# Splitting the first MLP chunk's operands during attention, and weaving the last mixing by a list

## The chip, the cores and the metric

The kernel runs on one core of a Trainium2 chip. The metric is the device time of one execution in microseconds. The engines are named as in the profile: PE (TensorE, matrix products) with PEld (its weight loads), DVE (VectorE), ACT (ScalarE), POOL (GpSimd) and SP (SyncE, which here only issues DMAs).

## The reference

Random-feature attention, then a token-mixing and channel MLP block, all in float32 (the MLP's weights arrive as float64).

```python
def phi(x):                       # x = q or k, scaled by D ** -0.25
    h = einsum('bhsd,md->bhsm', x, omega) - sum(x * x) / 2
    return exp(h - max(h)) / sqrt(m)
kv = einsum('bhsm,bhsd->bhmd', phi(k), v);  z = sum(phi(k), axis=2)
attn = einsum('bhsm,bhmd->bhsd', phi(q), kv) / (phi(q) . z + 1e-6)

x = attn as (8, 576, 512)
u = x + ((x.transpose(0, 2, 1) @ U) @ V).transpose(0, 2, 1)     # "mixing": U (576, 32), V (32, 576)
out = u + relu(u @ w_ch1) @ w_ch2                                # w_ch1 (512, 2048), w_ch2 (2048, 512)
```

Batch 8, 8 heads, 576 tokens, head width 64, 128 features.

## The kernel before, in words

Products of the MLP and of the feature projection are made from two-part operands: a high half (a copy to the type fp32r, on ACT) and a low half (the rest, a subtraction on DVE or POOL). Three products replace one: high x high, high x low, low x high. "Splitting" a tile means making these two halves; the function `split` (L735 to L738) does it in the MLP.

**Attention** (L638 to L720) is one software pipeline of 16 rounds of 9 steps, plus 7 steps to drain it; `s` is the step. A step handles one tile of 128 rows for two parts, a key unit and a query unit: project (PE, L528 to L530), row maximum `nm` (DVE, L536), exponentials `e` (ACT, L543), then kv products for keys (L440), or transposes (L466), a copy `eT` (L471) and the products with kv (L479, L486) for queries; `finish` divides and writes the result into the tile `x` (L496 to L511). The loads of a round are issued one round earlier by SP: `kt` and `qt`, 8 DMAs each (L381), and the values (L423, L427).

Four pairs of batches are formed. When a pair's x is complete, a generator `mixing` (L279) is put in a queue and advanced twice per step. It makes `py` (5 tiles, twice; PE L327) from the halves `mh` (ACT, L290) and `ml` (POOL, L291), copies it as `y` (ACT L330, DVE L332), then per tile a second product `ph` (`spread`, PE L302, L299), adds x (`add`, DVE L306, into one of two tiles `ut`) and stores the row tile u to device memory (SP, L312). The last pair's generator is not finished when attention ends.

A second generator, `decoding` (L106), turns the float64 words of U, V and the MLP's weights into float32 during attention: a load (three ahead), one or two ACT operations, five DVE operations (L142 to L150) and one on POOL (L167) per job. It is advanced in two steps of three until ten jobs are through (`left`). The rest of it is advanced in the first MLP chunk.

The **MLP** runs over chunks of token tiles: chunk 0 has six (768 tokens), the next ones four. Chunk 0 is computed plainly: for each of 16 slices f of the hidden width, `whole1` (L863) makes the first layer (12 products 512 wide and 12 products 256 wide, L876), `relu` the two halves of the activation (L885, L886), and `second` (L935) the second layer (L951). Chunks 1 and up use seven products per block pair in place of eight (`products`, L925).

In between stands the turn that the change touches. During attention the first six row tiles of u are loaded back transposed in blocks (`ahead`, L617; DMA L353) into four tiles and turned on DVE (`turn_ahead`, L627) into `uT` and three-buffered `us`. After attention (L987 to L999):

```python
weave()
ws[0] = Halves(0, nc.vector)      # split the first weights: ACT and DVE
one.whole(0)                      # split u, part 0: ACT and DVE
while not hold[0]:                # advance the last mixing to its 8th py tile
    weave()
for i in range(1, NC):
    one.whole(i)                  # split u, parts 1 to 3
for x in first_left:
    one.short(x)                  # split the 256 further tokens: ACT and POOL
```

and then the first pass, with one step of the mixing after each group of three products, the second with two (`twice`), and `settle` (L1006), which ends the mixing and frees its memory. Instructions wrapped in `tc.keep_in_program_order` (short: `keep`, `order`) are issued in the written order on their engine; others may be reordered by the scheduler, which orders by its own model of times when the program is built. Each engine works its list in order.

Of the kernel before, what the change touches and what calls it, by code (L numbers as in the profile page):

```python
# [9 lines left out]
F32 = mybir.dt.float32  # L10
F32R = mybir.dt.float32r
# [3 lines left out]
ALU = mybir.AluOpType  # L15
# [14 lines left out]
def performer_mlp_kernel(ctx: ExitStack, tc, q, k, v, omega, U, V, w1, w2, out):  # L30
# [27 lines left out]
    def f32(ap):  # L58
        return ap.bitcast(F32)
# [28 lines left out]
    tp = ctx.enter_context(tc.tile_pool(name="tp", bufs=1))  # L88
# [177 lines left out]
    left = [6 + 5 * EARLY]  # L266
# [10 lines left out]
    hold = [False]  # L277

    def mixing(pair, x, last):  # L279


        xs, ys, sums, stores = {}, [], {}, []
        rest = nc.gpsimd
        order = tc.keep_in_program_order if last else lambda step: step

        def prep(t):
            if t < NT:
                xh = mp.tile([P, DM], F32R, name="mh", bufs=2)
                xl = mp.tile([P, DM], F32R, name="ml", bufs=2)
                order(nc.scalar.copy(out=xh, in_=x[:, t, :]))  # L290
                order(rest.tensor_tensor(out=xl, in0=x[:, t, :], in1=f32(xh), op=ALU.subtract))  # L291
                xs[t] = (xh, xl)

        def spread(t):
            bank = "p_kv" if last and t % 2 else "p_m"
            sums[t] = ps.tile([P, DM], F32, name="ph", tag=bank)
            if t == 4:
                for b in range(2):
                    nc.tensor.matmul(sums[t], svm[:, b, :], ys[b], start=(b == 0), stop=(b == 1))  # L299
            else:  # L300
                b, r = divmod(t * P, S)
                nc.tensor.matmul(sums[t], sv[:, r : r + P], ys[b], start=True, stop=True)  # L302

        def add(t):
            ut = mp.tile([P, DM], F32, name="ut", tag="ut", bufs=2)
            order(nc.vector.tensor_tensor(out=ut, in0=sums.pop(t), in1=x[:, t, :], op=ALU.add))  # L306
            stores.append((u_rows(pair * NT + t), ut))

        def store():
            if stores:  # L310
                o, i = stores.pop()
                order(nc.sync.dma_start(out=o, in_=i))  # L312

        prep(0)
        yield
        yield
        for b in range(2):
            py = ps.tile([P, DM], F32, name="py", tag="p_m")
            for t in range(4 * b, 4 * b + 5):
                store()  # L320
                if (b, t) != (0, 4):
                    prep(t + 1)
                hold[0] = last and b == 1 and t > 6
                yield
                w = su[:, t + b, :, :].rearrange("p a r -> p (a r)")
                for i in range(2):
                    nc.tensor.matmul(py, w, xs[t][i], start=(t == 4 * b and i == 0), stop=(t == 4 * b + 4 and i == 1))  # L327
                yield
            y = mp.tile([P, DM], F32R, name="y", tag="y", bufs=2)
            order(nc.scalar.copy(out=y, in_=py))  # L330
# [12 lines left out]
        yield  # L343
        yield
        store()
# [268 lines left out]
    AFTER = 88  # L614
    first_uT, first_left, first_raw = [], [], {}

    def ahead(i):  # L617

        i //= 4
        if i == 0:  # L620
            first_uT.append(tp.tile([P, NC, TOK], F32, name="uT"))
        if i % 2 == 0:
            first_left.append(tp.tile([P, 2, TOK // 2], F32, name="us", bufs=3))
        first_raw[i] = rawp.tile([P, ends[0] * P], F32, name=f"raw{i}")
        fetch(0, {i: first_raw[i]})

    def turn_ahead(i):  # L627
        i, over = divmod(i, 2)
        o, x = first_uT[0][:, i, :], first_raw[i][:, :TOK]
        if over:  # L630
            o, x = first_left[i // 2][:, i % 2], first_raw[i][:, TOK:]
        tc.keep_in_program_order(nc.vector.transpose(o, x))

    steps = {}
    decoder = decoding([u_job(), *v_jobs(), *weight_jobs()], 6, EARLY)
    mixers = []
    x = None
    for s in range(NR * NT + 7):  # L638
# [17 lines left out]
        if AFTER <= s < AFTER + 4 * NC and (s - AFTER) % 4 == 0:  # L656
            ahead(s - AFTER)
# [60 lines left out]
        if mixers:  # L718
            next(mixers[0], 0)
        steps.pop(s - max(DELAY.values()), None)  # L720
# [6 lines left out]
    rows_out = out.rearrange("b s c -> (b s) c")  # L727
    up = ctx.enter_context(tc.tile_pool(name="up", reuse_waits="tile", bufs=2))
# [66 lines left out]
    class Halves:  # L795


        def __init__(self, f, rest=nc.gpsimd):
            self.ops = []
            for d in range(2):  # L800
                self.ops.append(weight_tile())
                split(self.ops[-1], w1f[:, 2 * d : 2 * d + 2, f * P : (f + 1) * P], rest)

    class Chunk:
        def __init__(self, c, raws=None):
            self.c, self.raws, self.turned, self.ops, self.s = c, raws or {}, 0, [], {}
            self.n = ends[c] - first[c]
            self.u, self.po = {}, None
            self.uT = tp.tile([P, NC, TOK], F32, name="uT") if c else first_uT[0]
            self.half = []  # L810

# [14 lines left out]
        def slot(self):  # L826
            self.ops.append(up.tile([P, 2, 2, HT], F32R, name="ux", bufs=8))
            return self.ops[-1]

        def whole(self, i):  # L830

            split(self.slot(), self.uT[:, i, :].rearrange("p (k t) -> p k t", k=2), nc.vector)

        def short(self, x, rest=nc.gpsimd):

            self.half.append(up.tile([P, 2, 2, HT], F32R, name="ux", bufs=8))
            split(self.half[-1], x, rest)
# [15 lines left out]
        def add(self):  # L853
# [5 lines left out]
            split(self.slot(), x, nc.gpsimd if self.c == 1 and i in (3, 5) else nc.vector)  # L859
# [127 lines left out]
    weave = lambda: next(mixers[0], None)  # L987
    while left[0] > 0:
        advance(decoder)
    weave()  # L990
    ws[0] = Halves(0, nc.vector)
    one.whole(0)
    while not hold[0]:
        weave()
    for i in range(1, NC):
        one.whole(i)
    for x in first_left:
        one.short(x)
    g = one.whole1(ws.pop(0), lambda: 1 in ws or ws.update({1: Halves(1)}), weave)  # L999
    late = {}  # L1000

    def twice():
        weave()
        weave()
# [11 lines left out]
    def whole_pass(chunk, g, each):  # L1016


        for f in range(NF):
# [3 lines left out]
            if f + 1 < NF:  # L1023
                places = iter(range(4))
                opening = chunk is one and f == 0
                g = chunk.whole1(ws.pop(f + 1), lambda: each(f, next(places)), twice if opening else lambda: None)
# [126 lines left out]
```

## Time and profile before

| | us |
|---|---|
| median of 3 runs | 1107.28 (1104.17 to 1108.17) |
| the profiled execution | 1106.08 |
| its span on the core | 1104.3 |
| mean granted PE clock | 0.992 |
| attention, first projection to last product | about 9 to 316 |
| the turn | about 316 to 341 |
| chunk 0, f = 2 and on | 344 to 461 |
| the other chunks | 461 to the end |

Rows of the profile are read thus: start, duration, engine, line, operation, output<-inputs, tile size and, in brackets, the idle time of that engine just before it with what ended it. "SPq" is SP's DMA issue. The windows give, for a stretch, its length, the busy time of each engine with the number of instructions, the granted PE clock (1.00 is full), the DMA engines' busy share and GB/s. PE's products overlap, so the distance between two starts, not the duration, is what a product costs.

### The profile page before, as it was taken

How to read it: one execution, taken by the hardware profiler on the slowest of the kernel's cores; microseconds unless marked ns; L12 is line 12 of the kernel's file. 1: busy time of each engine (PE TensorE's matmuls, PEld its weight loads, DVE VectorE, ACT ScalarE, POOL GpSimd, SP SyncE). 2: the span in 40 equal slices, each digit the busy share in tenths (PEclk: the TensorE clock that was granted, in tenths of full speed). 3: DMA queues.
4: the chain of work that ended last, by engine and by line, in shares of the span. 5: the costliest groups of instructions: out<-in, count | busy, mean ns of one | idle time of the engine just before them, and what ended most of it. 6: DMA issues, size and time to landing. Idle time of an engine off the chain costs nothing.

```text
span 1104.3 us, 20594 instructions
## 1 busy us (share of the span) xinstructions
PE 1083.6 (98%) x7119; PEld 978.1 (89%) x7119; DVE 684.3 (62%) x1484; ACT 500.4 (45%) x1405; POOL 335.7 (30%) x339
## 2 busy tenths in 40 slices
PE   9999999999989999999999999999999999999998
PEld 8899988999977878889898898888898888888987
DVE  4799999898977777565743643643643643643421
ACT  5789878888864665343421311311311312222232
POOL 3346547446363555665400100100100100100133
PEclk9899999999989999999999999999999999999999
DMA  8679888875204464475686786785785785785510
GB/s 136 140 145 158 166 188 152 167 152 90 87 9 154 134 158 100 135 248 191 219 252 173 219 253 162 223 256 153 228 260 160 220 265 160 209 264 163 181 58 20
DMA packets 344583, 187.93 MB, mean 170 GB/s; under 512 B 276128, under 2 KB 276128, under 8 KB 344480
## 3 DMA queue, kind: packets, MB, share of 16 engines
q1 hardware_dynamic: 342112, 186.32, 63.5%
q8 instruction: 57, 0.93, 0.4%
q10 hardware_dynamic: 2368, 0.30, 0.2%
q14 instruction: 46, 0.38, 0.1%
HBM read 152.99 MB, written 33.55 MB: 169 GB/s over the span
## 4 chain that ended last, share of the span: by engine, by line
PE 83%; DVE 6%; DMA 3%; ACT 3%; SPq 2%; issue 1%; POOL 1%; DVEq 0%; ACTq 0%; POOLq 0%
PE p_s L925 24%; PE p_n L951 17%; PE p_q L951 15%; PE p_p L876 6%; PE p_n L486 3%; PE p_kv L440 3%; PE p_p L528 3%; PE p_p L529 2%; PE p_p L530 2%; PE p_q L466 2%; SPq L381 2%; PE py L327 2%; DMA raw<-in_moe_w_ch_dram 1%; DMA kt<-in_k_dram 1%; DVE nm L536 1%
## 5 line engine op out<-in xcount | busy, mean ns | idle before, releaser
L925 PE MATMUL p_s<-ux,wx 128*128 128x256 f32 x2352 | 492.2, 279 | 0.9 <-DVE near L741 0.4
L925 PEld LDWEIGHTS p_s<-ux,wx 128*128 128x128 f32 x2352 | 436.8, 188 | 43.2 <-DVE near L741 0.7
L951 PE MATMUL p_n<-w2h,g 128*128 128x512 f32 x576 | 219.2, 395 | 0.5 <-DVE u L972 0.5
L951 PE MATMUL p_q<-w2h,g 128*128 128x512 f32 x512 | 195.8, 393 | 0.0
L543 ACT ACTIVATE e<-p_p,nm 128x128 f32<-128x128 f32 x576 | 167.0, 385 | 36.8 <-DVE nm L536 27.0
L409 POOL TENSOR_TENSOR xl<-xT,xh 128x384 fp32r<-128x384 f32 x95 | 99.9, 1068 | 135.2 <-ACT xh L405 106.8
L885 ACT ACTIVATE g<-far 128x256 fp32r<-128x256 f32 x112 | 46.8, 418 | 170.2 <-DVE far L741 170.2
L841 POOL TENSOR_TENSOR us<-uT 128x512 f32<-128x512 f32 x14 | 19.0, 1359 | 337.6 <-DVE uT L820 337.6
L951 PEld LDWEIGHTS p_n<-w2h,g 128*128 128x128 f32 x576 | 108.9, 189 | 10.4 <-issue 0.7
L951 PE MATMUL p_n<-w2l,g 128*128 128x512 f32 x288 | 114.0, 396 | 0.0
L741 DVE TENSOR_TENSOR near<-p_s,near 128x256 f32<-128x256 f32 x168 | 70.3, 418 | 67.0 <-PE p_s L925 65.7
L536 DVE TENSOR_REDUCE nm<-p_p 128x4 f32<-128x512 f32 x144 | 97.9, 680 | 22.1 <-PE p_p L530 16.9
L886 DVE SCALAR_TENSOR_TENSOR g<-p_s,g 128x256 fp32r<-128x256 f32 x56 | 23.7, 424 | 139.8 <-ACT g L885 139.8
L738 POOL TENSOR_TENSOR wx<-w1f,wx 128x256 fp32r<-128x256 f32 x86 | 68.3, 809 | 135.8 <-ACT wx L737 134.1
L885 ACT ACTIVATE g<-p_s 128x256 fp32r<-128x256 f32 x56 | 21.6, 385 | 185.6 <-PE p_s L925 185.6
L951 PEld LDWEIGHTS p_q<-w2h,g 128*128 128x128 f32 x512 | 96.4, 188 | 10.0
L876 PE MATMUL p_p<-ux,wx 128*128 128x256 f32 (+1 forms) x576 | 99.3, 324 | 3.1 <-DVE ux L738 2.4
L876 PEld LDWEIGHTS p_p<-ux,wx 128*128 128x128 f32 x576 | 88.2, 193 | 15.4 <-DVE ux L738 2.9
L951 PE MATMUL p_q<-w2l,g 128*128 128x512 f32 x256 | 100.3, 392 | 0.0
L528 PE MATMUL p_p<-omh,xh 128*128 128x256 f32 x288 | 93.7, 325 | 2.0 <-ACT e L543 1.7
L886 DVE SCALAR_TENSOR_TENSOR g<-far,g 128x256 fp32r<-128x256 f32 x112 | 49.5, 442 | 54.2 <-ACT g L885 54.2
L529 PE MATMUL p_p<-oml,xh 128*128 128x256 f32 x288 | 82.3, 286 | 0.0
(125 smaller groups left out, 1891.7 us busy)
## 6 DMA issues: line engine op xcount, KB each, us to landing
wx<-wx_dram SPq DMA_DIRECT2D x336, 256.0 KB, 3.2
raw<-in_moe_w_ch_dram SPq DMA_DIRECT2D x32, 512.0 KB, 4.2
wx_dram<-wx SPq DMA_DIRECT2D x56, 256.0 KB, 2.1
u_dram<-ut SPq DMA_DIRECT2D x36, 256.0 KB, 2.4
u<-u_dram SPq DMA_DIRECT2D x34, 256.0 KB, 4.4
out_dram<-u SPq DMA_DIRECT2D x34, 256.0 KB, 3.3
kt<-in_k_dram SPq DMA_DIRECT2D x120, 72.0 KB, 2.8
qt<-in_q_dram SPq DMA_DIRECT2D x120, 72.0 KB, 2.6
```

Source lines behind the costliest of these rows:

```text
L409: rest.tensor_tensor(out=self.xl[-1], in0=self.turned, in1=f32(self.xh[-1]), op=ALU.subtract)
L528: nc.tensor.matmul(o, part.xh[g][:, ts], oh, start=True, stop=False)
L529: nc.tensor.matmul(o, part.xh[g][:, ts], ol, start=False, stop=False)
L536: nc.vector.tensor_reduce(out=self.nm[:, :n], in_=self.pp[:, :n], axis=AX.X, op=ALU.max, negate=True)
L543: nc.scalar.activation(out=self.e[:, j, :], in_=self.pp[:, j, :], func=AF.Exp, bias=self.nm[:, j : j + 1])
L738: keep(rest.tensor_tensor(out=hl[:, 1], in0=x, in1=f32(hl[:, 0]), op=SUBTRACT))
L741: keep(nc.vector.tensor_tensor(out=out, in0=a, in1=b, op=op))
L876: nc.tensor.matmul(ph, l, r, start=(cc + i == 0), stop=(cc == NC - 1 and i == 2))
L885: keep(nc.scalar.activation(out=g[:, 0, ts], in_=x, func=AF.Relu))
L886: keep(nc.vector.scalar_tensor_tensor(out=g[:, 1, ts], in0=x, scalar=0.0, in1=f32(g[:, 0, ts]), op0=ALU.max, op1=ALU.subtract))
L925: tc.keep_in_program_order(nc.tensor.matmul(o, l, r, start=(i in (0, 1, 2, 5) and k + j == 0), stop=(k == 1 and j == 2), skip_group_check= ...
L951: tc.keep_in_program_order(nc.tensor.matmul(po, l, r, start=(begin and n + i == 0), stop=(end and n == len(fs) - 1 and i == 2)))
```

## The change

- A new pool `uxp`, allocated below the attention's pools, holds six operand tiles `ux`. The u operands of chunk 0 are split into it during attention. From step 91 on, each of the four parts takes 12 steps: load at 0 (one buffer instead of four), DVE transpose of 512 tokens at 7, its two halves (ACT, POOL) at 8, DVE transpose of the 256 further tokens at 10, its halves (ACT, POOL) at 11. `uT` and `us` (pool `tp`) are allocated after attention and serve chunks 1 and up.
- The first weights (f = 0) are split at step 144 on ACT and POOL, into the two buffers `ut`.
- The last mixing adds in place: `ut` is the tile of x itself, and the store reads x. Its first four `spread` products move up between the py products of the second half, on the bank `p_kv`. The low halves of tiles 6 and 8 are made on DVE, not POOL. After attention, PE's order of the mixing is fixed too, and the number of steps of the mixing after each group of first-layer products comes from a list.
- The decoder starts at step 10 instead of 1 and idles 4 calls instead of 6 before its first work; `left` is 4 + 50 instead of 6 + 50.
- Later chunks take two of eight operand tiles from a small pool `uy`, the other six from `uxp`.

```diff
-    tp = ctx.enter_context(tc.tile_pool(name="tp", bufs=1))
+    uxp = ctx.enter_context(tc.tile_pool(name="uxp", reuse_waits="tile", bufs=1))
...
-    left = [6 + 5 * EARLY]
+    left = [4 + 5 * EARLY]
...
-    hold = [False]
+    woven = []
...
+        place = lambda step: tc.keep_in_program_order(step) if woven else step
         def prep(t):
...
+                rest = nc.vector if last and t in (6, 8) else nc.gpsimd
                 order(rest.tensor_tensor(out=xl, in0=x[:, t, :], in1=f32(xh), op=ALU.subtract))
         def spread(t):
-            bank = "p_kv" if last and t % 2 else "p_m"
+            bank = "p_kv" if last and (t < 4 or t % 2) else "p_m"
...
         def add(t):
-            ut = mp.tile([P, DM], F32, name="ut", tag="ut", bufs=2)
+            ut = x[:, t, :] if last else mp.tile([P, DM], F32, name="ut", tag="ut", bufs=2)
...
+        early = 4 if last else 0
         for b in range(2):
             py = ps.tile([P, DM], F32, name="py", tag="p_m")
             for t in range(4 * b, 4 * b + 5):
                 store()
+                if t - 6 in sums:
+                    add(t - 6)
                 if (b, t) != (0, 4):
                     prep(t + 1)
-                hold[0] = last and b == 1 and t > 6
                 yield
                 w = su[:, t + b, :, :].rearrange("p a r -> p (a r)")
                 for i in range(2):
-                    nc.tensor.matmul(py, w, xs[t][i], ...)
+                    place(nc.tensor.matmul(py, w, xs[t][i], ...))
+                if b and t > 4 and t - 5 < early:
+                    spread(t - 5)
                 yield
...
             ys.append(y)
-            hold[0] = False
+            if b and early:
+                store()
+                add(early - 1)
             yield
             yield
-        for t in range(NT):
+        for t in range(early, NT):
...
-    AFTER = 88
+    AFTER, LATE = 91, 9
...
+    def operand():
+        return uxp.tile([P, 2, 2, TOK // 2], F32R, name="ux", bufs=6)
+    def ahead(i, what):
+        keep = tc.keep_in_program_order
+        ts = slice(0, TOK) if what < 10 else slice(TOK, None)
+        if what == 0:
+            first_raw[0] = rawp.tile([P, ends[0] * P], F32, name="raw")
+            fetch(0, {i: first_raw[0]})
+        elif what in (7, 10):
+            first_raw[1] = rawp.tile([P, TOK], F32, name="turned")[:, : TOK if what == 7 else TOK // 2]
+            keep(nc.vector.transpose(first_raw[1], first_raw[0][:, ts]))
+            if what == 7:
+                first_ops.append(operand())
+            elif i % 2 == 0:
+                first_half.append(operand())
+        elif what in (8, 11):
+            x, u = first_raw[1], first_half[-1] if what == 11 else first_ops[-1]
+            high, low = (... for a in range(2))
+            keep(nc.scalar.copy(out=high, in_=x))
+            keep(nc.gpsimd.tensor_tensor(out=low, in0=x, in1=f32(high), op=ALU.subtract))
...
-        if s % 3:
+        if s % 3 and s > LATE:
             advance(decoder)
-        if AFTER + 8 <= s < AFTER + 8 + 6 * NC and s % 3 == 2:
-            turn_ahead((s - AFTER - 8) // 3)
+        if AFTER <= s < AFTER + 12 * NC:
+            ahead(*divmod(s - AFTER, 12))
...
+        if s == NR * NT:
+            for d in range(2):
+                wt = mp.tile([P, 2, 2, P], F32R, name="wx", tag="ut", bufs=2)
+                tc.keep_in_program_order(nc.scalar.copy(out=wt[:, 0], in_=w1f[:, 2 * d : 2 * d + 2, 0:P]))
+                tc.keep_in_program_order(nc.gpsimd.tensor_tensor(out=wt[:, 1], ...))
+                first_wx.append(wt)
...
+        def slot(self, ops):
+            ops.append(up.tile([P, 2, 2, HT], F32R, name="uy", bufs=2) if slots[0] % 8 < 2 else operand())
+            slots[0] += 1
+            return ops[-1]
...
-    weave = lambda: next(mixers[0], None)
...
-    g = one.whole1(ws.pop(0), lambda: 1 in ws or ws.update({1: Halves(1)}), weave)
+    woven.append(True)
+    turns = iter((1, 2, 2, 2, 1, 1, 0, 0) + (2,) * 8)
+    def weave():
+        for _ in range(next(turns)):
+            next(mixers[0], None)
+    g = one.whole1(Halves(0, first_wx), lambda: 1 in ws or ws.update({1: Halves(1)}), weave)
```

More of the change, by code (lines that the diff above doesn't have):

```diff
@@ L342, in mixing @@
             add(t)
-        yield
-        yield
-        store()
+        while stores:
+            store()
+            yield
     def fetch(c, raws):
@@ L613, in performer_mlp_kernel @@
     }
-    AFTER = 88
[L615 to L632, printed above, removed]
+    AFTER, LATE = 91, 9
+    first_wx = []
+    first_ops, first_half, first_raw = [], [], [None, None]
+    def operand():
[15 more added lines that the diff above has]
+            x, u = first_raw[1], first_half[-1] if what == 11 else first_ops[-1]
+            high, low = (u[:, a, i % 2] if what == 11 else u[:, a].rearrange("p k t -> p (k t)") for a in range(2))
+            keep(nc.scalar.copy(out=high, in_=x))
+            keep(nc.gpsimd.tensor_tensor(out=low, in0=x, in1=f32(high), op=ALU.subtract))
     steps = {}
-    decoder = decoding([u_job(), *v_jobs(), *weight_jobs()], 6, EARLY)
+    decoder = decoding([u_job(), *v_jobs(), *weight_jobs()], 4, EARLY)
     mixers = []
@@ L795, in performer_mlp_kernel, with __init__ @@
     class Halves:
-        def __init__(self, f, rest=nc.gpsimd):
-            self.ops = []
-            for d in range(2):
+        def __init__(self, f, ops=None):
+            self.ops = ops or []
+            for d in range(0 if ops else 2):
                 self.ops.append(weight_tile())
-                split(self.ops[-1], w1f[:, 2 * d : 2 * d + 2, f * P : (f + 1) * P], rest)
+                split(self.ops[-1], w1f[:, 2 * d : 2 * d + 2, f * P : (f + 1) * P])
+    slots = [0]
     class Chunk:
@@ L808, in __init__ @@
             self.u, self.po = {}, None
-            self.uT = tp.tile([P, NC, TOK], F32, name="uT") if c else first_uT[0]
             self.half = []
+            if c:
+                self.uT = tp.tile([P, NC, TOK], F32, name="uT")
+            else:
+                self.ops, self.half = first_ops, first_half
         def fetch(self):
@@ L824, in block @@
             return self.uT[:, 2 * d : 2 * d + 2, t * HT : (t + 1) * HT]
[L826 to L832, printed above, removed]
+        def slot(self, ops):
+            ops.append(up.tile([P, 2, 2, HT], F32R, name="uy", bufs=2) if slots[0] % 8 < 2 else operand())
+            slots[0] += 1
+            return ops[-1]
         def short(self, x, rest=nc.gpsimd):
-            self.half.append(up.tile([P, 2, 2, HT], F32R, name="ux", bufs=8))
-            split(self.half[-1], x, rest)
+            split(self.slot(self.half), x, rest)
         def sum(self, i, a, b, op, out=None):
@@ L1025, in whole_pass @@
                 opening = chunk is one and f == 0
-                g = chunk.whole1(ws.pop(f + 1), lambda: each(f, next(places)), twice if opening else lambda: None)
+                g = chunk.whole1(ws.pop(f + 1), lambda: each(f, next(places)), weave if opening else lambda: None)
                 if opening:
```

31 lines of the change are left out of this document (9 added, 22 removed).

## The prediction

> **What bounds the kernel now.** I read the page first (busy shares, clock row, chain), then the windows by stage, then the order of time inside the stage that stands out.
>
> ```profile
> span 1104.3 us, 20594 instructions
> PE 1083.6 (98%) x7119; PEld 978.1 (89%) x7119; DVE 684.3 (62%) x1484; ACT 500.4 (45%) x1405; POOL 335.7 (30%) x339
> PEclk9899999999989999999999999999999999999999
> PE 83%; DVE 6%; DMA 3%; ACT 3%; SPq 2%; issue 1%; POOL 1%; DVEq 0%; ACTq 0%; POOLq 0%
> L536 DVE TENSOR_REDUCE nm<-p_p 128x4 f32<-128x512 f32 x144 | 97.9, 680 | 22.1 <-PE p_p L530 16.9
> ```
>
> TensorE (PE) is the bound: 83% of the chain, 98% of the span. Its clock row has two weak slices, the 2nd (27.6 to 55 us) and the 12th (304 to 331 us). The 144 rows of L536 count the attention steps. The windows price the two places:
>
> ```profile
> 33.00:60.00 27.00, 25.39 (x186) 24.15 (x187) 21.06 (x54) 20.70 (x69) 11.66 (x12) 0.87 0.73 134
> 200.00:300.00 100.00, 100.00 (x853) 97.58 (x852) 91.57 (x229) 84.09 (x275) 44.42 (x44) 1.00 0.57 125
> 315.73:341.42 25.69, 20.45 (x74) 15.54 (x75) 18.39 (x28) 10.32 (x22) 11.26 (x10) 0.80 0.20 75
> 344.15:460.97 116.82, 116.13 (x587) 98.27 (x586) 81.49 (x123) 66.14 (x137) 61.60 (x59) 1.00 0.47 132
> ```
>
> The columns are length, busy time of PE, weight loads, DVE, ACT, POOL, then the clock. From 200 us to the end of attention PE never idles; from 344 us on it idles 0.7 us in 117. The turn from attention to the MLP (315.73, last attention product done, to 341.42, the first p_q product of the second layer) has 5.2 us idle and a clock of 0.80. What PE has to do there comes from these rows:
>
> ```profile
> 344.15 4.32 PE L876 MATMUL p_p<-ux,wx 128*128 128x512 f32 x24
> 348.30 0.40 PE L951 MATMUL p_n<-w2h,g 128*128 128x512 f32 x1
> 348.54 0.40 PE L951 MATMUL p_n<-w2l,g 128*128 128x512 f32 x1
> 318.35 0.50 PE L327 MATMUL py<-ml,su 128*128 128x512 f32 x1 [0.78 <-POOL ml L291]
> 321.74 1.22 PE L876 MATMUL p_p<-ux,wx 128*128 128x512 f32 x2 [2.43 <-DVE ux L738]
> 322.75 0.63 PE L327 MATMUL py<-ml,su 128*128 128x512 f32 x1
> 323.18 0.63 PE L327 MATMUL py<-mh,su 128*128 128x512 f32 x1
> 335.56 0.50 PE L302 MATMUL ph<-y,sv 128*128 128x512 f32 x1 [0.79 <-DVE ut L306]
> 337.55 0.58 PE L302 MATMUL ph<-y,sv 128*128 128x512 f32 x1 [1.15 <-DVE ut L306]
> ```
>
> One first-layer pass (24 products) takes 348.30 - 344.15 = 4.15 us undisturbed; a 512-wide product starts 0.23 us after the last (348.30 to 348.54). After the stall of 2.43 us the same product takes 0.43 us (322.75 to 323.18): the clock is halved. The turn holds two passes (8.3 us), 10 products of the first mixing (L327), 10 of the second (L299, L302) and 6 of p_n, 26 x 0.23 = 6.0. Work 14.3 us, length 25.7: **11.4 us are lost**, and that is the most that this place can give. The idle times name the culprits: DVE splitting the u operands (ux), POOL's low halves (ml), DVE's sums into ut.
>
> **The change, part by part.**
>
> ```profile
> 317.79 2.21 DVE L738 TENSOR_TENSOR wx<-w1f,wx 128x256 fp32r<-128x256 f32 x2 [0.84 <-ACT wx L737]
> 319.93 5.72 DVE L738 TENSOR_TENSOR ux<-uT,ux 128x512 fp32r<-128x512 f32 x4
> 321.27 3.23 POOL L738 TENSOR_TENSOR ux<-us,ux 128x512 fp32r<-128x512 f32 x2
> 339.64 1.50 DVE L306 TENSOR_TENSOR ut<-ph,x 128x512 f32<-128x512 f32 x2 [1.33 <-DMA u_dram<-ut]
> 316.52 0.42 DVE L511 TENSOR_TENSOR x<-p_n,rec 128x256 f32<-128x256 f32 x1
> L738 DVE TENSOR_TENSOR ux<-uT,ux x26: 677/692/1758, 319.9 to 1043.0; 128x512 fp32r<-128x512 f32 x26
> L306 DVE TENSOR_TENSOR ut<-ph,x x36: 646/678/692, 127.4 to 340.4; 128x512 f32<-128x512 f32 x36
> L291 POOL TENSOR_TENSOR ml<-x,mh x36: 1272/1286/1723, 96.2 to 319.7; 128x512 fp32r<-128x512 f32 x36
> L738 POOL TENSOR_TENSOR wx<-w1f,wx x86: 729/739/1182, 328.9 to 1093.6; 128x256 fp32r<-128x256 f32 x86
> 319.02 1.65 ACT L737 CAST ux<-uT 128x512 fp32r<-128x512 f32 x3
> 317.36 0.70 ACT L737 CAST wx<-w1f 128x256 fp32r<-128x256 f32 x2
> L330 ACT CAST y<-py x8: 586/606/721, 110.3 to 326.0; 128x512 fp32r<-128x512 f32 x8
> ```
>
> *Splits out of the turn.* DVE loses 2.21 + 5.72 = 7.9 us, POOL 3.2, ACT its six ux casts and two wx casts. With them goes the 2.43 us stall and the half clock behind it.
>
> *The list, in place of hold.* Walking the generator, 18 of its stops pass inside attention in both versions; the rest is now laid between groups of three first-layer products (3 x 0.23 = 0.69 us wide; the twelve narrow ones have 4.15 - 12 x 0.23 = 1.4 us, so 0.35 a group). I follow the list from 315.73. py(4), py(5) and spread(0) reach 317.3, as now; group 0 to 318.0. py(6) waits for its low half, now on DVE behind the last norm (316.52 + 0.42): 0.69, done about 317.7, no stall to speak of. spread(1) waits for add(0), which stands behind that subtract: 318.4, so about 0.3 us lost. From there each spread has a group and a py (1.1 us) to cover the 0.68 add: covered, until DVE's subtract for tile 8 comes between add(1) and add(2); I put 0.5 us on py(8) and spread(3). After py(8) come y (ACT 0.61), its low half, add(3) and the low half of the wide relu, in this order on DVE, each taken at L306's 0.68 since all three read PSUM: with the hand-overs some 2.9 us after py(8). PE has spread(3), group 3 and the narrow half, 0.23 + 0.69 + 1.4 = 2.3, before it needs that relu's bank: 0.5 to 0.7 lost. Weights for f = 1 (ACT 0.70, POOL 2 x 0.74) come just behind the relu; half of it shows, 0.4. In the second pass spread(4) to spread(8) alternate between two banks with 0.92 us each: covered. Sum of stalls 2.0 us. The turn then takes 14.3 + 2.0 = 16.3 instead of 25.7: **9.4 us gained**. Bounds: 11.4 if nothing waits; 7.3 if both DVE subtracts take the longest of their row, 1.76 instead of 0.69, because POOL works beside them (2.1 us more). I take 9.4, since most DVE operations of the stretch read PSUM like L306, whose row never leaves 0.65 to 0.69.
>
> [...]
>
> *u added in place.* The sums no longer wait for a store to land (1.33 us at 339.64): inside the 9.4. What is late next is the store itself, reading x: nothing overwrites x before the w2 tiles of f = 2, several us later. No cost.
>
> *Splits into attention (s = 91 to 138).* ACT gains 4 wide casts at 0.55 and 4 narrow at 0.35, plus the two wx casts: 4.3 us. POOL gains 4 x 1.29 + 6 x 0.74 = 9.6. DVE's eight transposes were there already, each now followed one step later by its cast. The cover is ACT's 16 and POOL's 56 idle us in 200:300. If that cover holds, 0; if every ACT microsecond is exposed, 4.3; a gain is excluded because nothing leaves this stretch. I take 0.8: PE was 100.00 busy beside ACT at 84, so nearer to nothing. The 16 loads of u (SP) stay 16, now in four groups 12 steps apart with one buffer. Step time is (315.7 - 9.1)/144 = 2.1 us, so the transposes come 15 us after their load: no wait.
>
> *The decoder six steps later.*
>
> ```profile
> 20.25 5.30 SPq L381 DMA_DIRECT2D qt<-in_q_dram  x8
> 25.60 0.50 SPq L220 DMA_DIRECT2D raw<-in_moe_U_dram  x1
> 28.01 4.43 SPq L244 DMA_DIRECT2D raw<-in_moe_V_dram  x8
> 32.53 0.93 SPq L423 DMA_DIRECT2D x<-in_v_dram  x2
> 36.15 5.96 SPq L381 DMA_DIRECT2D kt<-in_k_dram  x8
> 47.09 0.99 SPq L423 DMA_DIRECT2D vt<-in_v_dram  x2
> 58.53 4.28 SPq L381 DMA_DIRECT2D qt<-in_q_dram  x8
> 35.06 0.41 PE L440 MATMUL p_kv<-x,e 128*128 128x65 f32 x2 [0.65 <-DMA x<-in_v_dram]
> 62.85 0.58 DVE L401 STREAM_TRANSPOSE xT<-qt 128x384 f32<-128x384 f32 x1 [0.91 <-DMA qt<-in_q_dram]
> ```
>
> SP issues without a pause here. The 12 loads of U and V (25.60 to 32.5, 6.9 us) stand ahead of the values of keys 2, and PE waits for these at 35.06. In 33:60 PE idles 1.6 us and runs at 0.87: 1.6 + 0.13 x 27 = 5.1 us, the upper bound. After the change those 12 go behind qt of round 2: values, kt and qt come 6.9 us sooner, but kt and qt of round 3 still have all of it in front (less one weight load, 0.5 to 0.6 us), and DVE waits for them at 62.85 already now. So the time won at 35 us is stood out again at 62: I take **0.7**, nearest to that row. Lower bound -1.6: the idle time returns there whole. The decode steps dropped from s = 10 to 15 return at s = 85 to 91, where the splits have hardly begun: nothing.
>
> *After the turn.* All from 341.42 on follows in the same order and only moves; u rows are stored earlier. The pool of six plus two uy tiles is the same rotation of eight. Nothing.
>
> **Sum.** The profiled execution took 1106.08 (span 1104.3), 1.2 below the median 1107.28 of three. 1106.1 - 9.4 - 0.7 + 0.8 = 1096.8; put on the median, 1098.0.
>
> **The rivals.**
>
> *A, the opening gives its all* (5.1 rather than 0.7): for it, the half clock would not begin at 37 us; against, 62.85. 1098.0 - 4.4 = 1093.6.
>
> *B, the added casts and low halves push the exponentials and xl of attention,* since they are held in order on both queues: 4.3 exposed on ACT and the turn at its lower bound 7.3: 1098.0 + 3.5 + 2.1 = 1103.6. Against it stands 100.00 of 100.
>
> *C, the fixed list runs as one serial chain and the kernel gets slower.* The PE order can't be evaded any more. If each of nine spreads waits for an add and its hand-over (0.68 + 0.2) and five py for cast and POOL subtract (0.6 + 1.29), that is 7.9 + 9.5 = 17.4 us of stalls, 31.7 in the turn, 6.0 above now: 1107.28 + 6.0 = 1113.3. It decides from 11.4 us of stalls. Against: most waits have 1.1 us of products between them, and casts run while POOL subtracts.
>
> *D, the gain is handed back later,* because the weights of f = 2 and after are decoded at their own pace: then PE idle after 341 grows by what the turn gave, 1106 to 1107. Against: the decode steps are tied to PE's order, and 344:461 idles only 0.7 us.
>
> **How the numbers follow.** Forecast 0.60 (own range 1095 to 1101), A 0.14, B 0.12, D 0.08, C 0.06. A measurement of this kernel tells about 0.5% (5.5 us) from no change: faster means below 1101.7. Forecast and A give 0.74; of B I count a fifth as still faster (0.03); same takes the rest of B and D, 0.16; slower is C and a little of D, 0.07. The range leaves out the far ends of A and of B, and C: 1092 to 1104.
>
> **What would show it.** Right: the turn, from the last attention product to the first p_q product, takes 15 to 18 us; no PE wait over 1 us on ux or ut; clock 1.00 throughout; the window of 100 us before it stays above 99 busy; DVE waits some us for qt near 60 us. Wrong: stalls of PE on ut or y in every group (C); PE idle on e with ACT full between 200 and 300 us (B); idle time on w2h or wx after the turn (D); clock 1.00 from 25 to 60 us with the round 3 loads in time (A).

## The result, and the profile after

| | before | after |
|---|---|---|
| median of 6 runs each, us | 1105.01 (1102.46 to 1108.17) | **1096.28** (1095.41 to 1097.94) |
| the profiled execution, us | 1106.08 | 1095.41 |
| its span on the core, us | 1104.3 | 1093.6 |

The ratio is 0.9916, 95% interval 0.9901 to 0.9932: faster by 9.3 us (7.5 to 10.9); the two medians of the table differ by 8.7. The forecast was 1098.0, which is 9.3 below the 1107.28 that it started from.

The page of the changed kernel: span, busy time of each engine, the clock row and the chain's shares by engine.

```profile
span 1093.6 us, 20576 instructions
PE 1075.1 (98%) x7119; PEld 972.8 (89%) x7119; DVE 678.3 (62%) x1480; ACT 498.9 (46%) x1407; POOL 338.4 (31%) x345
PEclk9999999999999999999999999999999999999999
PE 85%; DVE 6%; DMA 3%; ACT 2%; issue 2%; SPq 1%; POOL 1%; DVEq 0%; POOLq 0%; ACTq 0%
```

PE executes the same 7119 products; both weak slices of its clock row are gone. The windows of the same places as before (length; busy time of PE, weight loads, DVE, ACT, POOL; clock):

```profile
33.00:60.00 27.00, 25.28 (x219) 24.35 (x217) 21.60 (x58) 22.38 (x76) 11.07 (x11) 1.00 0.71 131
200.00:300.00 100.00, 99.09 (x836) 95.78 (x836) 90.11 (x227) 86.08 (x282) 51.91 (x50) 1.00 0.61 132
314.87:330.83 15.96, 14.82 (x75) 12.35 (x75) 11.56 (x23) 6.57 (x14) 5.12 (x6) 1.00 0.35 131
333.55:450.10 116.55, 116.24 (x591) 99.07 (x590) 81.29 (x124) 66.60 (x137) 62.41 (x59) 1.00 0.48 130
```

The third row is the turn, with the same two ends as before: 25.69 us have become 15.96. The spans differ by 10.7, and the ends of this window split that: the turn 9.73; the end of attention 0.86 (315.73 to 314.87); all the rest 0.11 (762.88 to 762.77, from the end of the turn to the end of the span). How much of the 9.73 an execution gets depends on the clock. The runs b1 and b2 below keep the old turn. These are their windows of it:

```profile
313.03:337.59 24.56, 19.31 (x75) 14.23 (x76) 18.27 (x27) 10.31 (x22) 11.29 (x10) 0.86 0.20 76
318.55:341.72 23.17, 17.92 (x74) 13.48 (x75) 17.18 (x25) 10.31 (x22) 11.27 (x10) 0.93 0.21 79
```

PE idles as long as in the kernel before (5.25 and 5.25 beside 5.24 us), but the clock is 0.86 and 0.93 instead of 0.80. The old turn thus took 23.2 to 25.7 us in three executions, and the profile before shows the longest. The second row of the windows after is the first surprise: between 200 and 300 us PE, which never idled there before, idles 0.9 us.

What is left of waiting in the turn, in order of time (start, duration, engine, line, operation; in brackets the idle time before it):

```profile
316.11 0.69 DVE L293 TENSOR_TENSOR ml<-x,mh 128x512 fp32r<-128x512 f32 x1
317.81 1.30 POOL L293 TENSOR_TENSOR ml<-x,mh 128x512 fp32r<-128x512 f32 x1 [1.91 <-PE py L331]
318.98 0.68 DVE L293 TENSOR_TENSOR ml<-x,mh 128x512 fp32r<-128x512 f32 x1
322.05 0.71 ACT L759 CAST wx<-w1f 128x256 fp32r<-128x256 f32 x2
322.41 0.69 DVE L308 TENSOR_TENSOR x<-ph,x 128x512 f32<-128x512 f32 x1
323.02 1.01 DVE L909 SCALAR_TENSOR_TENSOR g<-p_p,g 128x512 fp32r<-128x512 f32 x2
323.85 0.93 PE L899 MATMUL p_p<-ux,wx 128*128 128x512 f32 x3 [1.14 <-ACT wx L759]
```

PE has one wait, of 1.14 us at 323.85, where the prediction put the bank of the wide relu and the next weights. The profile names ACT's weight cast, yet the two casts for the second pass (the row at 322.05) had ended at 322.76, while DVE's low half of the relu (L909), behind the sum of L308, began at 323.02. Run v2 below decides between the two.

### The profile page after: what moved, and what is told of

Read it like the earlier page. It is cut to its first block, busy times and chain, and to the rows that moved or that the text cites. A ratio compares the mean times of both kernels' runs of the same rounds, so it can differ in the third digit from the quotient of the medians.

```text
span 1093.6 us, 20576 instructions
## 1 busy us (share of the span) xinstructions
PE 1075.1 (98%) x7119; PEld 972.8 (89%) x7119; DVE 678.3 (62%) x1480; ACT 498.9 (46%) x1407; POOL 338.4 (31%) x345
## 4 chain that ended last, share of the span: by engine, by line
PE 85%; DVE 6%; DMA 3%; ACT 2%; issue 2%; SPq 1%; POOL 1%; DVEq 0%; POOLq 0%; ACTq 0%
PE p_s L948 23%; PE p_n L974 17%; PE p_q L974 15%; PE p_p L899 8%; PE p_kv L448 3%; PE p_n L494 3%; PE p_p L536 3%; PE p_p L537 2%; PE p_p L538 2%; PE p_q L474 2%; PE py L331 1%; DVE nm L544 1%; ACT e L551 1%; PE p_m L974 1%; PE p_kv L974 1%
## 5 line engine op out<-in xcount | busy, mean ns | idle before, releaser
L948 PE MATMUL p_s<-ux,wx 128*128 128x256 f32 x1728 | 364.1, 280 | 0.9 <-DVE near L763 0.4
L948 PEld LDWEIGHTS p_s<-ux,wx 128*128 128x128 f32 x1728 | 321.5, 188 | 32.6 <-DVE near L763 0.7
L948 PE MATMUL p_s<-uy,wx 128*128 128x256 f32 x624 | 132.6, 279 | 0.0
L948 PEld LDWEIGHTS p_s<-uy,wx 128*128 128x128 f32 x624 | 117.1, 188 | 11.1
L909 DVE SCALAR_TENSOR_TENSOR g<-p_s,g 128x256 fp32r<-128x256 f32 x56 | 23.7, 424 | 139.4 <-ACT g L908 139.4
L536 PE MATMUL p_p<-omh,xh 128*128 128x256 f32 x288 | 92.8, 322 | 1.4 <-ACT e L551 0.9
L899 PE MATMUL p_p<-ux,wx 128*128 128x512 f32 (+1 forms) x480 | 84.8, 326 | 1.4 <-ACT wx L759 1.1
L899 PEld LDWEIGHTS p_p<-ux,wx 128*128 128x128 f32 x480 | 73.8, 190 | 10.8 <-ACT wx L759 1.3
```

The costliest lines, as they stand in the source:

```text
L536: nc.tensor.matmul(o, part.xh[g][:, ts], oh, start=True, stop=False)
L899: nc.tensor.matmul(ph, l, r, start=(cc + i == 0), stop=(cc == NC - 1 and i == 2))
L948: tc.keep_in_program_order(nc.tensor.matmul(o, l, r, start=(i in (0, 1, 2, 5) and k + j == 0), stop=(k == 1 and j == 2), skip_group_check= ...
```

## The experiments

The medians are of 4 to 12 executions each. Besides the time, two numbers are read from each trace: the length of the turn, and the **lead**, the start of the k-th step's first feature projection (first rows of L528, in the changed kernel L536) minus its start before, worked out from the timeline. Negative means earlier. The measured ratio is always to the kernel before.

| kernel | median us | ratio, 95% interval | turn | lead at step 15 | 54 | 72 | 84 | 96 | 108 | 141 |
|---|---|---|---|---|---|---|---|---|---|---|
| after | 1096.28 | 0.9916 (0.9901 to 0.9932) | 15.96 | -5.5 | -0.9 | -4.4 | -3.8 | -2.5 | -1.3 | -1.0 |
| b1 | 1102.98 | 0.9979 (0.9968 to 0.9991) | 24.56 | -6.4 | -1.5 | -4.2 | -3.7 | -2.3 | -2.7 | -2.7 |
| e1 | 1098.37 | 0.9937 (0.9918 to 0.9955) | 15.98 | -3.5 | +0.1 | -1.6 | -1.6 | -1.6 | +0.4 | +0.8 |
| e3 | 1101.65 | 0.9973 (0.9961 to 0.9984) | 15.99 | -3.4 | -0.1 | +2.9 | +2.9 | +5.4 | +7.0 | +7.4 |
| e2 | 1096.87 | 0.9923 (0.9909 to 0.9938) | 16.68 | -4.2 | -0.6 | -3.8 | -3.2 | -1.9 | -0.3 | +0.1 |
| e4 | 1096.36 | 0.9925 (0.9903 to 0.9946) | 16.01 | -2.2 | -0.5 | -3.6 | -3.1 | -1.8 | -0.5 | -0.1 |
| e6 | 1097.98 | 0.9937 (0.9917 to 0.9957) | 16.77 | -5.4 | -0.2 | -3.2 | -2.7 | -1.4 | +0.4 | +0.7 |
| e8 | 1099.75 | 0.9954 (0.9938 to 0.9971) | 19.12 | -2.5 | -0.4 | -2.5 | -1.9 | -0.6 | +1.1 | +1.5 |
| e5 | 1096.5 | 0.9927 (0.9909 to 0.9945) | 16.00 | -2.8 | -1.1 | -3.6 | -3.1 | -1.7 | -0.4 | -0.2 |
| b2 | 1109.5 | 1.0041 (1.0027 to 1.0054) | 23.17 | -0.8 | -0.9 | -1.3 | -1.3 | -1.3 | +2.5 | +2.8 |
| e7 | **1092.67** | 0.9891 (0.9871 to 0.9911) | 15.97 | -5.8 | -1.7 | -5.2 | -4.7 | -3.3 | -3.8 | -3.4 |
| v2 | 1094.2 | 0.9906 (0.9891 to 0.9920) | 15.37 | -2.4 | -0.2 | -3.7 | -3.2 | -1.8 | -2.3 | -1.9 |

A lead early in the kernel carries a clock episode or none (last section). At step 15, the kernels with the later decoder lead by 5.4 to 6.4 us where the opening ran at full clock, and by 2.2 to 2.8 where 3.4 us were lost to the clock. By step 54 the two groups overlap (0.2 to 1.7 and 0.2 to 1.1). Differences between leads within one execution, and medians, are therefore safer than one early lead.

### The opening: b1, e1, e3

b1 is the kernel before with the later decoder alone; e1 is the changed kernel with the decoder at its old place; e3 lets the decoder idle for eight calls.

```diff
 b1, on before
-    left = [6 + 5 * EARLY]            +    left = [4 + 5 * EARLY]
-    ... weight_jobs()], 6, EARLY)     +    ... weight_jobs()], 4, EARLY)
-        if s % 3:                     +        if s % 3 and s > 9:
 e1, on after:  left = [6 + 5 * EARLY], 6 idle calls, LATE = 0
 e3, on after:  left = [8 + 5 * EARLY], 8 idle calls
```

> The kernel before, with the decoder's later start as its only change (first call at step 10, 4 idle calls, left = 4 + 50). The changed kernel's steps run 5.5 us ahead of the kernel before at step 15, but only 0.9 ahead at step 54 and 1.0 at the end of attention. Theory T (the time won at 35 us is waited out again at 44 and 58 us): 0 to 1.5 us faster than before, the lead at step 15 near 5 us and below 2 us by step 54. Rival R1 (the later start is worth 3 to 5 us for good, and it is the splits added to attention that eat it): 3 to 5 us faster, the lead of 3 us or more kept to step 140.

> The changed kernel, with the decoder starting as before (step 1, 6 idle calls, left = 6 + 50); all else as changed. T: 0 to 1.5 us slower than the changed kernel, so 7.5 to 9 us faster than before; the turn stays at 16 us. R1: 3 to 5 us slower than the changed kernel, so 4 to 6 us faster than before.

> The changed kernel with 8 idle calls of the decoder instead of 4 (left = 8 + 50): the loads start at the same step, the first work on them 6 steps later. In the changed kernel ACT waits 1.9 us for U at 43.5 us with the exponentials behind it, and PE 1.25 us. T: this wait goes, and the lead is waited out at qt of the third round instead: 0 to 1 us faster than the changed kernel. Rival: the wait is worth its PE time and more: 1.5 to 3 us faster than the changed kernel. Rival on the other side: the decoder now ends at step 97, inside the splits, and DVE is slower there: 1 to 2 us slower.

b1 gives 2.3 us (1.0 to 3.5), and e1 lacks 2.3 of what the whole change gives (0.9937 beside 0.9916, though these two intervals overlap): the later decoder is worth about 2.3 us, in both kernels. That is between the forecast 0.7 and rival A's 5.1, and between the two ranges expected of b1 and e1. The lead shows the course that was predicted, time won early and stood out again: b1 is 6.4 us ahead at step 15 and 1.5 at step 54. But the course does not end there. All nine kernels with the later decoder and four idle calls win another 2.1 to 3.5 us between steps 54 and 72 (e1 1.7, b2 0.4), and all nine lose 1.8 to 1.9 again between steps 72 and 96 (e1 and b2 nothing). So what is left at the end is not what is left of the opening. Where the early lead goes is in the opening of the changed kernel:

```profile
25.54 0.99 SPq L431 DMA_DIRECT2D x<-in_v_dram  x2
29.16 4.32 SPq L389 DMA_DIRECT2D kt<-in_k_dram  x8
39.26 0.50 SPq L220 DMA_DIRECT2D raw<-in_moe_U_dram  x1
41.62 4.04 SPq L244 DMA_DIRECT2D raw<-in_moe_V_dram  x8
43.54 0.49 ACT L123 ACTIVATE mag<-raw 128x320 f32<-128x320 f32 x1 [1.91 <-DMA raw<-in_moe_U_dram]
44.34 0.33 PE L474 MATMUL p_q<-ident,e 128*128 128x128 f32 x1 [1.25 <-ACT e L551]
58.89 0.58 DVE L409 STREAM_TRANSPOSE xT<-qt 128x384 f32<-128x384 f32 x1 [1.07 <-DMA qt<-in_q_dram]
```

The values and kt go out 7 us earlier than before (25.54 for 32.53, 29.16 for 36.15). The wait for qt stays, as forecast (1.07 at 58.89). But a wait that I did not list is larger: ACT's first decode operation stands 1.91 us for U at 43.54, with the exponentials behind it in its order, and PE stands 1.25 for an e.

So e3, which delays that operation by four calls (six steps), should have gained. It lost 5.3 us to the changed kernel instead; all 12 of its runs (1100.56 and up) lie above the slowest of after (1097.94). No theory had this size; one rival had 1 to 2 us, for the decoder's end among the splits. The trace, of an execution 2.1 us above the median, has a lower clock in three places. Of the rows below all are from e3 but the last, which is from the kernel before:

```profile
24.00:40.00 16.00, 14.26 (x112) 13.96 (x111) 9.12 (x18) 11.44 (x40) 5.25 (x6) 0.89 0.79 137
76.00:84.00 8.00, 6.68 (x45) 6.32 (x44) 6.13 (x17) 5.79 (x21) 2.17 (x2) 0.79 1.06 198
150.00:166.00 16.00, 14.25 (x95) 13.70 (x96) 11.77 (x30) 9.51 (x31) 5.24 (x5) 0.79 0.89 189
155.12 0.72 PE L474 MATMUL p_q<-ident,e 128*128 128x128 f32 x2 [1.70 <-ACT e L551]
153.31 0.69 DVE L308 TENSOR_TENSOR ut<-ph,x 128x512 f32<-128x512 f32 x1 [1.94 <-DMA u_dram<-ut]
156.41 0.69 DVE L306 TENSOR_TENSOR ut<-ph,x 128x512 f32<-128x512 f32 x1 [1.09 <-DMA u_dram<-ut]
```

Time at a lower clock adds up to 16 x 0.11 + 8 x 0.21 + 16 x 0.21 = 6.8 us, but that is not the +7.4 of the lead. The first episode is not the edit's (e2, e4, e5, e8 and v2 lose 1.7 or 3.4 us there too), and at step 54 e3 stands at -0.1. Against after, the largest piece is 4.5 us between steps 63 and 72, the third place. It begins with a store: a sum of the first pair's mixing waits 1.94 us for the store of its buffer, the row maxima and the exponentials stand behind it, and PE's 1.70 at 155.12 follows. The kernel before waits 1.09 for a store at this place; b1 and after do not. That goes with what they win between steps 54 and 72, though no run isolates it. The decoder's operations now fall four calls later against the mixing of the first two pairs; how that moves the stores was not isolated either.

### The turn: e2, e4, e6, e8, v2

e2 takes away the list and the early spreads, e6 the adding in place, e4 the low halves on DVE, e8 all three, so that the splits in attention stand alone. v2 moves one sum behind the low half of the wide relu (on top of e7, below).

```diff
 e2:  bank = "p_kv" if last and t % 2 ..., early = 0, no woven.append(True),
      one weave() of three stops ahead of the pass, then 1 per group, in the second pass 2
 e4:  rest = nc.gpsimd
 e6, a free x tile as two buffers of sums:
+            if last and not own:
+                own.append(xp.tile([P, NT, DM], F32, name="x"))
+            ut = own[0][:, t % 2, :] if last else mp.tile(...)
 e8:  e2, e4 and e6 together
 v2, on e7:  add(early - 1) moved from ahead of the first yield after ys.append(y) to behind it
```

> The changed kernel with its splits in attention, but the last mixing as before: run up to its 8th py tile ahead of the first pass, then one step per group of three products and two in the second pass, no spreads between the py products, PE's order free. T (splits and list share the gain): the stall on ux (2.43 us) and the half clock behind it stay away, the sums' hand-overs return: the turn takes 18 to 21 us instead of 16.0 (before 25.7), so 4 to 7 us faster than before. Rival (the list gives it all): turn 24 us or more. Rival (the splits give it all): turn 16 to 17 us.

> The changed kernel, with the low halves of tiles 6 and 8 on POOL as the others (1.28 us each instead of DVE's 0.69). If POOL's price counts: tile 6's, 7's and 8's halves follow one another on POOL, PE waits 0.5 to 1.5 us on py, the turn takes 16.5 to 17.5 us. Rival (DVE and POOL hold each other up, so DVE's share is worth nothing): 16 us, as in the changed kernel.

> The changed kernel, with the sums of the last mixing written to two buffers in turn (in a free tile), as in the kernel before, not in place. If the in-place sum is part of the gain: sums wait again for stores to land (before: 0.5 and 1.3 us in the turn), the turn takes 17 to 18.5 us instead of 16.0, 1 to 2.5 us slower than the changed kernel. Rival (the list spaces the sums by more than a store takes): 16 to 16.5 us.

> The changed kernel with only the splits moved into attention: the last mixing woven as before (run to its 8th py tile, one and two steps, free PE order), sums into two buffers in turn, all low halves on POOL. Without the list alone the turn took 16.7 us, without the in-place sums 16.8. If the parts add up: 17.4 to 18 us, 7 to 8 us faster than before. Rival (each of the two covers for the other): 19 to 21 us.

> In place for all pairs (as e7) and, in the turn, the sum of tile 3 after the low half of the wide relu on DVE. In the changed kernel the second pass starts 1.14 us late, at 323.85, behind DVE's 0.69 for tile 3 and the relu's low half. If the bank that the relu frees is what it waits for: the wait falls to 0.4 to 0.6 us, the turn to 15.3 to 15.5 us. Rival (it waits for the second slice's weights, as the profile names it): 16.0 us, no change against e7.

The splits alone bring the turn from 25.69 to 19.12 us: 6.6 of the 9.7. The other three together bring the further 3.2, but each taken away by itself costs only 0.7 (e2), 0.05 (e4) and 0.8 (e6): they take the place of one another. The times of these kernels agree in order (e8 0.9954, e6 0.9937, e2 0.9923), but only e8 is clearly slower than after by the intervals. Against the expectations, e2 (16.68), e4 (16.01) and e8 (19.12) came out in the range of the rival and e6 (16.77) between the two ranges. The turn of e8, three waits of PE and two of DVE:

```profile
319.90 0.50 PE L334 MATMUL py<-ml,su 128*128 128x512 f32 x1 [0.82 <-POOL ml L294]
331.89 0.50 PE L305 MATMUL ph<-y,sv 128*128 128x512 f32 x1 [0.87 <-DVE x L311]
333.88 0.50 PE L305 MATMUL ph<-y,sv 128*128 128x512 f32 x1 [1.13 <-DVE x L311]
329.41 0.69 DVE L311 TENSOR_TENSOR x<-ph,x 128x512 f32<-128x512 f32 x1 [0.42 <-DMA u_dram<-x]
335.96 1.49 DVE L311 TENSOR_TENSOR x<-ph,x 128x512 f32<-128x512 f32 x2 [1.33 <-DMA u_dram<-x]
```

These are the waits of before (0.78 on ml, 0.79 and 1.15 on the sums; on DVE 0.50 and 1.33 on stores), without the 2.43 on ux and without the half clock. e8 writes its sums to two buffers in turn as before, so its sums wait for stores too. Which of PE's waits come from that is shown by e2, which adds in place and has no such wait. Its rows:

```profile
328.13 0.68 DVE L909 SCALAR_TENSOR_TENSOR g<-p_p,g 128x512 fp32r<-128x512 f32 x1
329.18 0.43 DVE L143 TENSOR_SCALAR mag<-mag 128x512 uint32<-128x512 uint32 x1
329.52 2.63 DVE L308 TENSOR_TENSOR x<-ph,x 128x512 f32<-128x512 f32 x4
330.26 0.50 PE L304 MATMUL ph<-y,sv 128*128 128x512 f32 x1 [1.14 <-DVE x L308]
```

The longer of the two waits on sums stays in e2 (1.14 us), so it is no wait for a store. It is one for DVE's order: the sum stands behind the low half of the relu and the decoder's operations. The shorter one (0.87 in e8) is gone in e2; the two buffers are its likely source, which no run isolates. With early spreads, a list and sums in place (after) both are gone. The 1.33 us for a store, which the prediction counted for the sums in place, hold no product: in e8 as in before PE runs on without a wait behind its last spread.

v2 settles the last wait of after. Its first-layer products after the wide relu, and the low half of that relu:

```profile
322.28 0.93 PE L900 MATMUL p_p<-ux,wx 128*128 128x512 f32 x3 [0.55 <-ACT g L909]
321.44 0.69 DVE L910 SCALAR_TENSOR_TENSOR g<-p_p,g 128x512 fp32r<-128x512 f32 x1
```

With the sum behind the low half, 1.14 us fall to 0.55 and the turn to 15.37, as expected. In both kernels the product starts 0.83 to 0.84 us after the low half does (323.85 and 323.02, 322.28 and 321.44). So the wait at 323.85 was for the bank that DVE's low half frees, not for the weights on ACT that the profile names.

### Attention: e5, b2, e7

The lead of the changed kernel falls from 3.8 to 1.3 us between steps 84 and 108, when the u operands are loaded and split; b1, which has no splits there and its loads at the old places, loses 1.0. Two suspects: the added casts and subtractions, or the loads moved to new places. e5 executes each high and each low half twice. b2 is the kernel before with the loads and transposes of u laid as in the change (one buffer, 12 steps apart), without splits. e7 adds u in place for all pairs, so that no sum of any mixing waits for the store of one of two buffers.

```diff
 e5, on after, in ahead()
-            keep(nc.scalar.copy(...))             +            for _ in range(2): keep(nc.scalar.copy(...))
-            keep(nc.gpsimd.tensor_tensor(...))    +            for _ in range(2): keep(nc.gpsimd.tensor_tensor(...))
 b2, on before
-        first_raw[i] = rawp.tile(..., name=f"raw{i}")    +        first_raw[i] = rawp.tile(..., name="raw")
-        if AFTER <= s < AFTER + 4 * NC and (s - AFTER) % 4 == 0: ahead(s - AFTER)
+        if 91 <= s < 91 + 12 * NC and (s - 91) % 12 == 0: ahead((s - 91) // 3)
-        ... s % 3 == 2: turn_ahead((s - AFTER - 8) // 3)
+        ... (s - 91) % 12 in (7, 10): turn_ahead((s - 91) // 12 * 2 + ((s - 91) % 12 == 10))
 e7, on after
-            ut = x[:, t, :] if last else mp.tile(...)    +            ut = x[:, t, :]
```

> The changed kernel, with each of the eight splits in attention done twice in a row (each ACT copy twice, each POOL subtraction twice): the suspected cost doubled, 3.6 us more on ACT and 8.1 more on POOL. In the changed kernel the lead over the kernel before falls by 2 us in steps 90 to 108, where the first part is split; parts two to four cost nothing that the steps show. Theory S (the price is the u loads and stores that now queue on SP beside the second pair's mixing, not the splits): 0 to 0.5 us slower than the changed kernel. Rival (the splits crowd ACT and POOL): 1 to 2 us slower or more.

> The kernel before, with the loads of u alone moved as in the changed kernel (one buffer, four groups 12 steps apart from step 91, transposes at 7 and 10 steps behind); no split is moved and the decoder starts as before. Theory S: both signs, as in e1: 1 to 2 us won by step 72, since the 12 loads that stood on SP between 165 and 194 us are gone, and 1 to 2 us lost in steps 96 to 108, where a group of loads now stands between the stores of the second pair; in sum 0 to 0.5%, not to be told from the kernel before. Rival (the loss in steps 96 to 108 belongs to the splits): won by step 72 and kept, 1.5 us faster.

> The changed kernel with u added in place for all four pairs, so that no sum waits for a store of its buffer to land. In the changed kernel DVE waits 0.2, 0.3 and 1.3 us for such stores at 219 to 227 us. S: these waits go and with them most of the 2 us lost in steps 90 to 108: 1 to 2 us faster than the changed kernel. Rival: what is lost there are the splits: no change.

Doubling the eight splits, 3.6 us more on ACT and 8.1 on POOL by the prediction's prices, makes no difference that can be told (0.9927 beside 0.9916; the intervals leave room for 1 to 2 us), and the loss between steps 84 and 108 is 2.7 beside 2.5. It is not the splits. The loads by themselves make the kernel before slower, 1.0041, though in the profiled execution its turn is 2.5 us shorter by the clock. Its loss between the two steps is 3.8 us where 1 to 2 were expected, 1.7 of it a lower clock at 232 us. (After the turn b2 is 2.3 us longer as well, 765.18 for 762.88; that is not explained.)

SP, DVE and ACT of the changed kernel at the second group of loads:

```profile
219.36 0.46 SPq L314 DMA_DIRECT2D u_dram<-ut  x1
220.56 1.73 SPq L361 DMA_DIRECT2D raw<-u_dram  x3
222.40 0.92 SPq L314 DMA_DIRECT2D u_dram<-ut  x1
223.36 0.43 SPq L361 DMA_DIRECT2D raw<-u_dram  x1
223.89 1.95 SPq L431 DMA_DIRECT2D vt<-in_v_dram  x2
226.75 0.69 DVE L308 TENSOR_TENSOR ut<-ph,x 128x512 f32<-128x512 f32 x1 [1.31 <-DMA u_dram<-ut]
228.13 2.20 ACT L551 ACTIVATE e<-p_p,nm 128x128 f32<-128x128 f32 x8 [1.96 <-DVE rec L504]
```

A mixing is under way there, and its stores stand in SP's list between the loads. A sum must wait until the store of its buffer has landed (1.31 at 226.75). It stands in DVE's order ahead of the row maxima, so the exponentials wait (1.96), and then PE. DVE's largest waits between 205 and 240 us (line, releaser: total, times, longest), first of after, then of e7, and PE's window of the same stretch in after and in e7:

```profile
DVE ut L308 <- DMA u_dram<-ut: 1.8, 3, 1.3
```

```profile
DVE nm L544 <- ACT e L551: 0.6, 2, 0.4
```

```profile
205.00:240.00 35.00, 34.19 (x294) 33.01 (x292) 32.21 (x82) 28.07 (x94) 14.72 (x15) 1.00 0.80 174
```

```profile
205.00:240.00 35.00, 35.00 (x306) 34.50 (x306) 33.77 (x87) 30.21 (x102) 15.86 (x16) 1.00 0.77 166
```

In e7 the wait is gone, and PE never idles: 306 products begin there, in after 294 (before 305). The loss between steps 84 and 108 falls from 2.5 to 0.9 us. The other kernels agree. Every one with the moved loads and two buffers of sums loses 2.0 to 4.1 us between these steps (after, e1 to e6, e8, b2); b1, e7 and v2 lose 0.9 to 1.0. DVE's waits for such stores between 195 and 245 us are 1.3 to 2.2 us in after, e2 to e5, e8 and b2, and none in before, b1, e7 and v2. (In e1 and e6 a wait of a sum, 1.7 and 2.2 us, stands in this stretch too, but the profile puts it down to PE.) The profiled e7 reaches the end of attention 2.5 us ahead of after, and its median is 3.6 us lower, where 1 to 2 were expected. The two intervals overlap by 0.001, but e4 and e5, timed beside e7 and with the turn of after, give the closer comparison: all four runs of e7 (up to 1093.58) lie below all ten of theirs (1094.78 and up). So the wait for the store is shown as the cause, by the trace and by taking it away; how much more than the 1.6 us between these steps it costs is not resolved. e7 beats both kernels by its median: 1092.67 us, ratio 0.9891. v2 can't be told from it by the intervals (0.9906).

## Why the prediction was right, point by point

**The turn** was forecast at 16.3 us and took 15.96: gain 9.7 for 9.4. The work stayed at 14.3 us and the stalls were 1.7 instead of 2.0, but the list of stalls was half wrong. The 0.3 us at spread(1) and the 0.5 on py(8) and spread(3) did not occur. The bank of the wide relu, put at 0.5 to 0.7, takes 1.14. The 0.4 for the weights of f = 1 showed nowhere as a wait of its own. So the sum is right partly because errors cancel. It was also counted against the slowest of three old turns: against their mean, 24.5 us, the gain is 8.5. The splits as main cause (the 2.43 us and the half clock) are shown by e8; the list and the sums in place are worth less than their place in the diff suggests, each having the other as a cover.

**The lower bound of the gain, 7.3 us,** was hardly put to the test. It takes DVE's two subtractions at 1.76 us each. In the profile before, three of the four at 319.93 took that (1.75, 1.76, 1.76), begun while POOL worked, and the fourth, begun at 324.97 after POOL's had ended at 324.50, took 0.68. In the changed kernel the two took 0.69 and 0.68 us, but the second lay beside POOL's (317.81 to 319.11) for only 0.13 us. In e2 it lay beside POOL's for 0.42 us (318.58, POOL to 319.00) and took 0.97, longer than either, and far from the 1.76 of the bound. e4 shows that it hardly matters for the turn where they run (16.01 beside 15.96).

**"The time won at 35 us is stood out again at 62"** was right, and even in size up to step 54: the nine kernels with the later decoder lead by 0.2 to 1.7 us there, 0.8 in the mean, where 0.7 was taken. The half clock of that window in before, priced in the upper bound, comes and goes between executions (the same code lost nothing in after and 3.4 us in e4) and is mostly stood out as well. Half of the sign of rival A, full clock from 25 to 60 us, thus showed in the profile after without A's gain; the loads of round 3 were not in time (1.07 at 58.89). In all 2.3 us stay (b1, and e1 against after), inside the bounds. What failed is "nothing" for the rest of attention: 2.1 to 3.5 us more are won between steps 54 and 72, and 1.8 to 1.9 lost between 72 and 96, in part where the decode steps return.

**"0.8 for the splits in attention"** put a cost to a wrong cause and at half its size. The splits cost nothing that shows (e5). The step that failed is "the 16 loads of u stay 16 ... no wait": it asked only whether the transposes wait for the loads, not what else stands in SP's list behind them. There it was the stores of another pair's u, and through the buffers of `ut` DVE, ACT and PE. From leads at step 141, after (-1.0) stands 1.7 us behind b1 (-2.7), the same decoder without the moved loads and splits, and 1.5 of that arises between steps 84 and 108; the profiled e7 regains that and more.

**"u added in place: no cost"** held for the last mixing, at a gain of 0.8 us in the turn (e6), though not by the 1.33 us that it names (e8). The remark that nothing overwrites x soon also held; that the same edit would pay more in the other mixings was missed.

**After the turn nothing**: 762.88 to 762.77 us. Rival D is out, and so are C (no chain of stalls in the turn) and B (e5, and a turn that gained 9.7).

The parts add up roughly: 9.7 (turn) + 2.3 (decoder) - 1.7 (loads in attention) = 10.3 us, or 9.1 with the mean old turn, beside 9.3 measured (7.5 to 10.9). The forecast total of 9.3 is thus closer than its terms deserve: the decoder gave 1.6 more than forecast, the loads took 0.9 more. That they nearly cancel is luck.

## What to carry to other kernels

When a DMA is moved, look along the queue that issues it for the stores that will now stand behind it, and ask which buffer each of them holds. Loads moved among a mixing's stores cost more here (1.6 us between steps 84 and 108, by e7) than 12 us of added ACT and POOL work on engines with room (nothing that shows, in e5). When several edits aim at the same stall, take each away alone and all together; only the pair of answers shows that one would nearly have done. And to start work later is no better for being later: after four of the decoder's calls more the kernel was 5 us slower.

## What the runs showed of the hardware

In these traces the granted clock falls after waits that are short one by one, and not after every wait of the same length. Before the low stretch in the opening of the kernel before, PE's longest single wait was the 0.65 us at 35.06 that the prediction quotes. These are two of its neighbours, and windows of the stretch that follows:

```profile
33.05 0.39 PE L528 MATMUL p_p<-omh,xh 128*128 128x256 f32 x1 [0.54 <-ACT e L543]
35.77 0.88 PE L440 MATMUL p_kv<-x,e 128*128 128x65 f32 x6 [0.30 <-DMA x<-in_v_dram]
...
37.00:39.00 2.00, 1.81 (x9) 1.62 (x9) 0.43 (x1) 2.00 (x8) 0.17 (x2) 0.61 0.70 118
39.00:41.00 2.00, 2.00 (x12) 2.00 (x12) 0.91 (x2) 1.50 (x6) 0.78 (x1) 0.50 0.24 37
43.00:45.00 2.00, 2.00 (x15) 2.00 (x14) 1.26 (x4) 1.54 (x5) 0.13 (x1) 0.68 0.87 139
```

The clock stands at one half while PE is busy all the time (0.50 from 39 to 41 us), and no single wait ahead of it is over 0.65 us; the four from 33.05 to 37.50 add up to 1.7. In these runs the length of one wait does not decide. After 0.95 us at 26.81 (e5) the clock fell. After 1.25 us at 44.34 (after), 1.30 at 43.55 (b1) and 1.51 at 45.24 (e6) it stayed at 1.00. The time lost, (1 - clock) x length summed over the opening, is about nothing (after, b1, e6, e7), 1.7 us (e1, e2, e3) or 3.4 us (before, b2, e4, e5, e8, v2), that is 3.4 or 6.8 us at half clock. The old turn lost 5.1, 3.4 and 1.6 us in before, b1 and b2, near multiples of the same size. Executions of one opening differ: PE waited 0.59 us at 27.18 in after and lost nothing, while in e4, the same code up to the turn, it waited 1.68 us at 27.45 and lost 3.4 us at 28 to 35 us. So a start read early in one profile is uncertain by about 3 us; by step 54 most of that is stood out again. Which wait brings on a fall, and why one opening loses nothing, 1.7 or 3.4 us from one execution to the next, was not shown.
